# Small column tiles for the first products, and two held projections ahead of the last eight output products

## The chip, the cores and the metric

The kernel runs on one core of a Trainium2 chip. The metric is the device time of one execution in microseconds (us); of several executions the median is given. The core has a matrix engine (TensorE, PE in the profile; PEld are its weight loads), VectorE (DVE), ScalarE (ACT), GpSimd (POOL) and SyncE (SP), which here issues most transfers. Each engine works through a list of instructions of its own, in order, and waits on semaphores for the others. Products write to PSUM, which DVE and ACT read.

## The reference

The input x has 2,048 tokens of 640 values. It is layer-normalised, and the result feeds two branches, whose product is added to x:

```python
xn = _layernorm(x, axis=-1)
s = _A_ref(xn, A_wq, A_wk, A_wv, A_wo, A_beta)     # attention with a memory
g = _silu(_B_ref(xn, B_w_gate, B_w_up, B_w_down))  # gated linear unit, F = 1536
return x + s * g
```

Branch A projects xn to q, k and v (32 heads of 20), and goes through four segments of 512 tokens. In a segment each head has causal softmax attention within the segment, and reads a memory that sums phi(k) v over the earlier segments; the two are mixed by a gate for each head, and the heads are projected by wo. Branch B is (sigmoid(xn w_gate) * (xn w_up)) w_down.

## The kernel before

The work goes by the four segments. For each there are the Q, K and V projections, the scores and their exponentials, the attention products, the memory, 12 gate and 12 up products of 128 columns of F each (`do_gate`, `do_up`), and the down projection in eight items (`do_down`: a block j of 128 tokens by a half of the 640 columns; 12 products that accumulate in a tile `yp`, then a Tanh on ACT and a DVE instruction at L449 that leaves `aa`, the silu). The output projection is in eight pieces of the same kind (five products over chunks c of 128 of the attention output `oT`, in a tile `sp`); a DVE instruction multiplies it with `aa`, and another adds x.

The order of instructions is written by the program itself, on the host: slots with due times (`TIMES`), and a list of dense work (`dense`) from which `step` takes one product at a time to fill the slots. `do_down` is a generator, and each `next` issues one product. Products of 32 columns of weights (`tile_position`) are used in some slots: four of them, one for each quarter of the columns, take the place of a full product (L128 instead of L124).

Tiles in PSUM with the tag "d" (`yp`, `sp`, `po`, `gp`, `up` and others) come from one pool, `ps_d`, of four buffers that are given out in turn. So a tile can be written only when the reader of the tile four allocations before it is done.

*The start.* `keep_warm(9)` issues nine products of zeros, `warm` (named `mn` in the profile), into a tile `wps` that nobody reads. Behind them on PE are the transposes of the first 128 tokens (`first_transpose`, L650), which wait for their normalised row `xn` on DVE; DVE and ACT compute mean, variance, root and `xn` for the four blocks of 128 tokens as these land. The transposes of the second block (L257) and the V projections follow.

*The end.* The last two items of the down projection of the last segment (j = 3, both halves) are kept back in `held`; held[1] is the first half and held[0] the second. The last chunk of `oT` is put together late: `tail_T4` transposes a part of the attention output on PE (`po`, two products), copies it on ACT (L517) and adds the other part, `o6`, on DVE (L518), for two token blocks at a time. The chunk before it is complete only after a transfer (`tail_load`, L507) and a DVE addition at L481. Nine products of the first held item are issued, then `tail_T4(0, 2)`, the item's last three products, two output pieces (`tail_piece`, L525 and L527), and the addition and store of block 0 (`tail_add`, L533 and L536). Then the same with the second held item and `tail_T4(2, 4)`, and then the other six pieces. POOL adds blocks 0 and 2, DVE blocks 1 and 3; SP issues the stores of blocks 0, 1 and 3, ACT those of block 2.

Of the kernel before, what the change touches and what calls it, by code (L numbers as in the profile page):

```python
# [15 lines left out]
L = 512  # L16
# [59 lines left out]
def kernel(  # L76
# [14 lines left out]
    nc = tc.nc  # L91
# [56 lines left out]
    warm = stg.tile([P, 3 * L], BF, name="mn")  # L148
# [98 lines left out]
    def ln_tiles(n):  # L247
        mv = lnp.tile([P, 4, 2], F32, name="mv")
        rs = lnp.tile([P, 4], F32, name="rs")
        return mv, rs  # L250
# [202 lines left out]
    def finish(steps):  # L453
        for _ in steps:
            pass
# [54 lines left out]
    def tail_T4(j0, j1):  # L510
        po = ps_d.tile([P, 2, P], BF, name="po", tag="d")
        for j in range(j0, j1):
            nc.tensor.transpose(po[:, j - j0, :], seg[NSEG - 1]["odot"][:, j, C4:D], ident[:])
        t = slice(j0 * P, j1 * P)
        oT = seg[NSEG - 1]["oT"][:, DC - 1, t]
        pf = po[:].rearrange("p j t -> p (j t)")
        nc.scalar.copy(oT[HALF:P, :], pf[HALF:P, :])  # L517
        nc.vector.tensor_tensor(oT[0:HALF, :], pf[0:HALF, :], o6[:, t], op=ALU.add)  # L518

    def tail_piece(j, half):  # L520

        s, hs = seg[NSEG - 1], slice(half * HD, (half + 1) * HD)
        sp = ps_d.tile([P, HD], F32, name="sp", tag="d")
        for c in range(DC):
            nc.tensor.matmul(sp[:], lhsT=s["oT"][:, c, j * P:(j + 1) * P], rhs=Wo[:, c, hs],  # L525
                             start=(c == 0), stop=(c == DC - 1), skip_group_check=True)
        nc.vector.tensor_tensor(s["aa"][j][:, hs], s["aa"][j][:, hs], sp[:], op=ALU.mult)  # L527

    def tail_add(j, h0, h1, eng, queue=None):

        hs = slice(h0 * HD, h1 * HD)
        xr = xt_of[NSEG - 1][:, j, hs]
        eng.tensor_tensor(xr, seg[NSEG - 1]["aa"][j][:, hs], xr, op=ALU.add)  # L533
        if queue is not None:
            t0 = (4 * (NSEG - 1) + j) * P
            queue.dma_start(o2[t0:t0 + P, hs], xr)  # L536
# [86 lines left out]
    wps = ps_d.tile([P, L], F32, name="wps", tag="d")  # L623

    def keep_warm(k):
        for _ in range(k):
            nc.tensor.matmul(wps[:], lhsT=warm[:, 0:P], rhs=warm[:, 0:L], start=True, stop=True)

    keep_warm(9)
    mv, rs = ln_tiles(0)  # L630
    new_seg(0)
    xns, sts = {}, {}
# [110 lines left out]
    held = [dense.pop() for _ in range(2)]  # L743
# [13 lines left out]
    for p in range(0, OLD, 5):  # L757
        n, g = units[p][0], units[p][1][0][0]
# [130 lines left out]
    def fill(want):  # L889
        while done < want and (cur[0] is not None or dense and may(dense[0][0])):  # L890
            step()
# [26 lines left out]
        if cur[0] is not None and cur[0][0] * cur[0][1] < TIMES["rest"]:  # L918
            complete()
    fill(1e12)  # L920
    for _ in range(9):
        next(held[1][3])
    tail_T4(0, 2)
    finish(held[1][3])
    tail_piece(0, 0)
    tail_piece(0, 1)
    tail_add(0, 0, 2, nc.gpsimd, nc.sync)
    for _ in range(9):
        next(held[0][3])
    tail_T4(2, 4)  # L930
    finish(held[0][3])
    tail_piece(1, 0)
    tail_piece(1, 1)
    tail_add(1, 0, 1, nc.vector)
# [38 lines left out]
```

## Time and profile before

| | us |
|---|---|
| median of 3 executions | 317.38 |
| lowest, highest | 317.27, 318.7 |
| the profiled execution, whole | 319.06 |
| its span, first to last instruction | 317.3 |
| PE busy in the span | 307.3 |
| ACT, DVE, POOL busy | 226.8, 224.8, 133.9 |
| first product of zeros | 1.24 |
| first transposes | 5.26 |
| first output piece of the tail | 305.07 |
| last store issued | 314.71 |

The profiled execution is one of its own, 1.68 us above the median. The span lies within its time; 1.76 us are around it. Times in the views of the profile count from the first instruction. A row of the timeline has the start, the time from the first start to the last end, the engine, the line, the operation with its tiles, the number of instructions and, in brackets, how long the engine stood idle before and what ended that. Products overlap in the pipeline: a single one of 320 columns takes 0.30 us from start to end, but the next one starts well before.

### The profile page before, as it was taken

To read this page: it belongs to the slowest core of one execution; us is meant where nothing else is said; L and a number is where in the kernel's file an instruction comes from. 1 tells how busy PE (TensorE), PEld (TensorE's weight loads), DVE (VectorE), ACT (ScalarE), POOL (GpSimd) and SP (SyncE) were. 2 spreads that over 40 slices of the span, in tenths; PEclk is the share of its full clock that TensorE was granted. 3 is DMA by queue.
4 is the path that set the end of the run, shared out by engine and by line. 5 is a ranking of instruction groups with operands and counts; after the bars stand their busy time and mean duration, and the time that the engine had idled before them with its cause. 6 is when DMAs were issued, how large, how long until landed. Compare 5 with 4: busy or idle time off the path is not lost.

```text
span 317.3 us, 10105 instructions
## 1 busy us (share of the span) xinstructions
PE 307.3 (97%) x4239; PEld 165.8 (52%) x4268; DVE 224.8 (71%) x507; ACT 226.8 (71%) x228; POOL 133.9 (42%) x231
## 2 busy tenths in 40 slices
PE   7999999999999999999999999999999999999985
PEld 2544445665445445654665455544466645445663
DVE  5474445665868988888778999788777777634565
ACT  3724477778798776777997869678896766777620
POOL 2870035535263445335443354454443353535312
PEclk9999999999999999999999999999999999999999
DMA  7984885420851362405953385137523001250202
GB/s 251 365 325 148 301 216 164 117 53 2 217 154 58 100 166 106 105 23 160 253 163 97 111 144 146 44 118 214 168 83 119 19 23 44 105 127 0 88 20 83
DMA packets 55245, 41.26 MB, mean 130 GB/s; under 512 B 25952, under 2 KB 53824, under 8 KB 55200
## 3 DMA queue, kind: packets, MB, share of 16 engines
q1 hardware_dynamic: 52656, 35.87, 39.5%
q10 hardware_dynamic: 2544, 4.75, 4.0%
q8 instruction: 33, 0.54, 0.7%
q14 instruction: 12, 0.10, 0.1%
HBM read 19.98 MB, written 14.73 MB: 109 GB/s over the span
## 4 chain that ended last, share of the span: by engine, by line
PE 91%; DMA 3%; DVE 2%; issue 1%; ACT 1%; SPq 0%; ACTq 0%
PE up L124 11%; PE gp L124 10%; PE psq L124 10%; PE yp L124 8%; PE Sps L541 8%; PE gp L128 6%; PE yp L128 6%; PE up L128 6%; PE ApsT L565 5%; PE psv L124 5%; PE psq L128 4%; PE sp L124 3%; PE sp L128 3%; PE psv L128 2%; PE sp L525 1%
## 5 line engine op out<-in xcount | busy, mean ns | idle before, releaser
L549 ACT ACTIVATE pt<-Sps 128x2048 bf16<-128x2048 f32 x80 | 150.3, 1878 | 40.8 <-PE Sps L541 40.0
L551 POOL TENSOR_SCALAR_AFFINE_SELECT pt<-pt 128x512 bf16<-128x512 bf16 x128 | 82.8, 662 | 156.7 <-ACT pt L549 156.7
L432 DVE SCALAR_TENSOR_TENSOR hT<-tg,up 128x512 bf16<-128x512 bf16 x48 | 32.6, 678 | 23.9 <-PE up L124 10.0
L124 PE MATMUL up<-xnT,Wu 128*128 128x512 bf16 x146 | 40.3, 380 | 1.4 <-issue 1.1
L124 PE MATMUL gp<-xnT,Wg 128*128 128x512 bf16 x146 | 38.9, 379 | 0.6 <-issue 0.5
L124 PE MATMUL yp<-Wd,hT 128*128 128x320 bf16 x246 | 38.5, 299 | 0.4 <-issue 0.4
L421 ACT ACTIVATE tg<-gp 128x512 bf16<-128x512 f32 x48 | 28.5, 595 | 14.3 <-PE gp L124 10.0
L541 PE MATMUL Sps<-QT,KT 23*128 23x384 bf16 (+3 forms) x512 | 31.8, 301 | 0.1
L124 PEld LDWEIGHTS <-hT 128*128 128x128 bf16 x246 | 22.7, 98 | 11.9 <-issue 3.6
L573 DVE STREAM_TRANSPOSE tb<-ApsT 128x512 f32<-128x512 f32 x31 | 22.0, 711 | 4.3 <-PE ApsT L565 4.2
L128 PE MATMUL gp<-xnT,Wg 128*32 128x512 bf16 x352 | 24.4, 380 | 0.0
L449 DVE SCALAR_TENSOR_TENSOR aa<-t,yp 128x320 bf16<-128x320 bf16 x32 | 15.3, 477 | 12.4 <-ACT t L448 12.2
L565 PE MATMUL ApsT<-pt,V 128*32 128x512 bf16 (+2 forms) x496 | 23.5, 299 | 0.0
L124 PEld LDWEIGHTS <-Wu 128*128 128x128 bf16 x159 | 14.2, 98 | 17.4 <-issue 4.0
L124 PEld LDWEIGHTS <-Wg 128*128 128x128 bf16 x152 | 14.1, 98 | 15.8 <-issue 1.9
L128 PE MATMUL yp<-Wd,hT 128*32 128x320 bf16 x552 | 21.9, 300 | 0.0
L128 PE MATMUL up<-xnT,Wu 128*32 128x512 bf16 x324 | 21.7, 380 | 0.0
L541 PEld LDWEIGHTS <-KT 23*128 23x128 bf16 x512 | 9.1, 92 | 23.5 <-issue 23.2
L585 DVE STREAM_TRANSPOSE obT<-ob 128x256 f32<-128x256 f32 x31 | 13.5, 434 | 11.1 <-POOL ob L582 11.1
L582 POOL TENSOR_TENSOR ob<-tb,rb 128x320 bf16<-128x320 f32 x27 | 19.9, 737 | 2.3
L124 PE MATMUL psq<-xnT,Wq 128*128 128x512 bf16 x82 | 19.4, 379 | 0.2
L124 PE MATMUL psv<-Wv,xnT 128*128 128x320 bf16 x115 | 18.6, 299 | 0.4 <-ACT xnT L655 0.2
(122 smaller groups left out, 441.0 us busy)
## 6 DMA issues: line engine op xcount, KB each, us to landing
KT<-Kd SPq DMA_DIRECT2D x32, 80.0 KB
QT<-Qd SPq DMA_DIRECT2D x32, 80.0 KB
out_dram<-xt SPq DMA_DIRECT2D x14, 160.0 KB
Wg<-in_B_w_gate_dram ACTq DMA_DIRECT2D x1, 1920.0 KB
Wu<-in_B_w_up_dram ACTq DMA_DIRECT2D x1, 1920.0 KB
xt<-in_A_x_dram SPq DMA_DIRECT2D x3, 640.0 KB
Wd<-in_B_w_down_dram SPq DMA_DIRECT2D x1, 1920.0 KB
Xd<-xn SPq DMA_DIRECT2D x12, 160.0 KB
```

The source lines that it names most:

```text
L124: nc.tensor.matmul(out_, lhsT=lhsT, rhs=rhs, start=start, stop=stop, skip_group_check=True)
L128: nc.tensor.matmul(out_[cols], lhsT=lhsT[:, cols], rhs=rhs, start=start, stop=stop, tile_position=(0, 32 * r), skip_group_check=True)
L421: nc.scalar.activation(tg[:], gp[:], ACT.Tanh, scale=0.5)
L432: nc.vector.scalar_tensor_tensor(out=h[:], in0=seg[n]["tg"][:], scalar=1.0, in1=up[:], op0=ALU.add, op1=ALU.mult)
L449: nc.vector.scalar_tensor_tensor(out=s["aa"][j][:, hs], in0=t2[:], scalar=1.0, in1=yp[:], op0=ALU.add, op1=ALU.mult)
L541: nc.tensor.matmul(Sps[:, r, c0:c0 + ncol], lhsT=KT[32 * r:32 * r + DH + 3, g, kb * P:(kb + 1) * P], rhs=QT[32 * r:32 * r + DH + 3, g, q0: ...
L549: nc.scalar.activation(pt[:, :, 0:ntot], Sps[:, :, 0:ntot], ACT.Exp, scale=SCALE)
L551: nc.gpsimd.affine_select(out=pt[:, :, c0:c0 + P], in_=pt[:, :, c0:c0 + P], compare_op=ALU.is_ge, fill=0.0, base=0, pattern=[[0, 4], [1, P ...
L565: nc.tensor.matmul(ps[32 * r:32 * r + 32, q0:L], lhsT=Vflat[n % 2][:, off:off + 32], rhs=t[:, r, c0:c0 + ncol], start=(i == 0), stop=(i == ...
L573: nc.vector.transpose(tb[:].rearrange("p h e -> p (h e)"), ps[:].rearrange("p (a t b) -> p a b t", t=32, b=2))
L582: eng.tensor_tensor(to, of, by, op=ALU.mult)
L585: nc.vector.transpose(s["obT", g // 4][:, g % 4, :].bitcast(F32), ob[:].rearrange("p a e b -> p (a e b)").bitcast(F32))
```

## The change

At the start the nine full products are replaced by 17 rounds of four products. Each of the four has 32 columns of the zero weights, streams 256 columns and writes its own 32 rows of `wps`. The one full product later on (`keep_warm(1)`) stays.

At the end both held items are completed, each with its `tail_T4`, before the first output piece. The held item that was first stays first. The eight pieces, the additions and the stores keep their order among themselves.

```diff
-    keep_warm(9)
+    def keep_warm_columns(k, n):
+        for _ in range(k):
+            for r in range(4):
+                nc.tensor.matmul(wps[32 * r:32 * r + 32, 0:n], lhsT=warm[:, 32 * r:32 * r + 32], rhs=warm[:, 0:n],
+                                 start=True, stop=True, tile_position=(0, 32 * r), skip_group_check=True)
+
+    keep_warm_columns(17, L // 2)
...
     fill(1e12)
-    for _ in range(9):
-        next(held[1][3])
-    tail_T4(0, 2)
-    finish(held[1][3])
+    for k in (1, 0):
+        for _ in range(9):
+            next(held[k][3])
+        tail_T4(2 - 2 * k, 4 - 2 * k)
+        finish(held[k][3])
     tail_piece(0, 0)
     tail_piece(0, 1)
     tail_add(0, 0, 2, nc.gpsimd, nc.sync)
-    for _ in range(9):
-        next(held[0][3])
-    tail_T4(2, 4)
-    finish(held[0][3])
     tail_piece(1, 0)
     tail_piece(1, 1)
```

## The prediction

> **What bounds the kernel now.** I read the page first, then the chain of waits, then the timeline at both ends of the execution, because the change touches only the first five microseconds and the last thirteen. The page's busy shares and slices:
>
> ```profile
> span 317.3 us, 10105 instructions
> PE 307.3 (97%) x4239; PEld 165.8 (52%) x4268; DVE 224.8 (71%) x507; ACT 226.8 (71%) x228; POOL 133.9 (42%) x231
> PE   7999999999999999999999999999999999999985
> ```
>
> TensorE (PE) is the bound: its slices are full but for the first and the last two. Something is to be had only there, and at most what PE stands idle. At the start (timeline of the first microseconds; columns: start, duration, engine, line, operation):
>
> ```profile
> 1.24 3.69 PE L627 MATMUL wps<-mn 128*128 128x512 bf16 x9 [1.24 <-DVE mn L149]
> 3.77 0.15 PEld L627 LDWEIGHTS <-mn 128*128 128x128 bf16 x1 [0.28 <-issue]
> 4.20 0.15 PEld L627 LDWEIGHTS <-mn 128*128 128x128 bf16 x1 [0.28 <-issue]
> 5.26 0.45 PE L650 MATMUL pT<-ident,xn 128*128 128x128 bf16 x5 [0.32 <-DVE xn L243]
> 6.05 0.49 DVE L637 BATCH_NORM_STATS2 st<-xt 128x6 f32<-128x320 bf16 x1 [0.21 <-DMA xt<-in_A_x_dram]
> 6.66 0.15 DVE L659 RECIPROCAL rs<-rs 128x1 f32<-128x1 f32 x1
> 7.35 0.45 PE L257 MATMUL pT<-ident,xn 128*128 128x128 bf16 x5
> ```
>
> The weight loads of the nine products come 0.43 us apart: 512 columns at half rate. The transposes at 5.26 take (0.45 - 0.22)/4 = 0.056 us each, which is full rate, so the rate doubled between 4.2 and 5.26. Products ahead of 5.25 do nothing for the result: the first transposes wait for xn, and the chain of waits through this stretch runs over the landing of an x tile at 6.03, DVE's statistics and xn to the transposes at 7.35.
>
> The end (timeline of the last microseconds):
>
> ```profile
> 304.67 0.57 PE L124 MATMUL yp<-Wd,hT 128*128 128x320 bf16 x3
> 305.07 0.57 PE L525 MATMUL sp<-Wo,oT 128*128 128x320 bf16 x3
> 305.76 0.43 DVE L481 TENSOR_TENSOR oT<-oT,oTm 128x512 bf16<-128x512 bf16 x1 [1.43 <-DMA oT<-OTd]
> 306.11 0.48 DVE L449 SCALAR_TENSOR_TENSOR aa<-t,yp 128x320 bf16<-128x320 bf16 x1
> 306.25 0.31 PE L525 MATMUL sp<-Wo,oT 128*128 128x320 bf16 x1 [0.60 <-DVE oT L481]
> 306.50 0.28 DVE L518 TENSOR_TENSOR oT<-po,o 64x256 bf16<-64x256 bf16 x1
> 306.70 0.47 DVE L449 SCALAR_TENSOR_TENSOR aa<-t,yp 128x320 bf16<-128x320 bf16 x1
> 306.83 0.99 PE L525 MATMUL sp<-Wo,oT 128*128 128x320 bf16 x6 [0.28 <-DVE oT L518]
> 307.66 1.39 PE L124 MATMUL yp<-Wd,hT 128*128 128x320 bf16 x9
> 309.40 4.24 PE L525 MATMUL sp<-Wo,oT 128*128 128x320 bf16 x30
> 313.00 0.49 DVE L527 TENSOR_TENSOR aa<-aa,sp 128x320 bf16<-128x320 bf16 x1 [0.19 <-PE sp L525]
> 314.38 0.33 DVE L533 TENSOR_TENSOR xt<-aa,xt 128x320 bf16<-128x320 bf16 x1
> ```
>
> The first output product (sp) does three of its five chunks and then stands: chunk 3 waits for a DMA and L481, chunk 4 for L518. Behind it on PE's queue is the second held down projection (yp, the nine at 307.66), which waits for nothing there. The end is then PE to 313.0, two DVE pairs (L527, L533), the last store issued at 314.71, and 2.6 us until the span ends.
>
> **The change at the start.** Removed: nine full products. Added: 17 sets of four products, each 32 columns wide, streaming 256 columns; PE gets 118 more instructions, the other queues none. What a set costs: in the middle of the kernel the same form runs, and 68 yp products in 32-column tiles take 2.49 us, which is (2.49 - 0.30)/16 = 0.137 us per set of four, against (1.39 - 0.30)/8 = 0.136 for one full product. The four run beside each other. At half rate a set of 256 columns is therefore half of the measured 0.427 us, 0.213; 17 sets are 3.63 us and end their streaming at 1.24 + 3.63 = 4.87. Nine full ones at half rate would have been 3.84, to 5.08. With the rate rising as before, somewhere in 4.2 to 5.26, both end sooner. Either way PE waits for xn until 5.25: cost nothing, with 0.38 us of cover. A further 0.35 us of delay would still be covered for the chain: the transposes' ACT copy stands ahead of the root of the second row (ACT 6.01 to 6.31), and DVE asks for that root at 6.66. Bounds: from below nothing, since the landing at 6.03 sets the chain whatever PE does; from above, if the four of a set ran one after another at half rate, 68 x 0.213 = 14.5 us, against which the measured 0.137 per set speaks; I take nothing.
>
> What it could touch is the clock. For column tiles as such the trace has a row: from 102.7 to 106.9 us PE runs only 32-column products and 23-row scores, is busy 4.20 of 4.20 us, and the granted clock is 1.00. That is holding the rate, not raising it; no row shows column tiles raising it.
>
> **The change at the end.** PE's order was: nine yp of the first held item, two transposes (po), three yp, sp(0,0), sp(0,1), nine yp of the second, two po, three yp, six sp. Now the second item goes in front of all eight sp. Work on PE is the same; what changes is who waits. A po takes 0.056, a yp or sp 0.136 (sp: (4.24 - 0.30)/29), results stand 0.30 after the last product's start, and a waiting engine starts 0.03 to 0.05 after its releaser. The tiles rotate over four PSUM buffers, so each allocation waits for the reader of the fourth before it.
>
> - Second item's nine yp start at 305.07 instead of the first sp (their buffer was free: sp(0,0) used it without a wait): 9 x 0.136, to 306.30.
> - The second pair of po takes the buffer that sp(0,1) had. Its last reader is L449 of the last planned down item, which stands on DVE behind L481's wait for the DMA and ends at 306.59. po waits, from 306.30 to 306.64, a new wait of 0.34 us; behind it on PE are the three yp: 306.75 to 307.16.
> - ACT: L517 of the second pair from 306.95 to 307.32 and the Tanh to 307.79; DVE: L518 second pair 307.35 to 307.63 (needs ACT's copy), L449 second item 307.82 to 308.31. DVE has nothing else to do then; L527 of sp(0,0) stands behind it and starts about 308.2, where before it ran at 307.18.
> - sp(0,0) takes the first held item's buffer: L449 of that item ends at 307.17, so sp starts at 307.22 (0.06 of waiting). Chunks 3 and 4 have been ready since 306.2 and 306.8. The third sp needs L449's end 308.31 at 308.58, the fifth L527's end 308.7 at 309.94: no more waits.
> - 40 sp at 0.136 run without a gap. The seventh one, sp(3,0), ends at 307.22 + 34 x 0.136 + 0.30 = 312.14, where it ended at 309.40 + 24 x 0.136 + 0.30 = 312.96. L527 starts at 312.17 instead of 313.00.
> - Behind it the same pairs on DVE and the same stores: last store issued at 313.88 instead of 314.71. POOL's first add slides from 308.43 to about 309.3 and its store on SP to 310.7, and its last two end about 312.9 with ACT's store behind them, 0.9 us ahead of the last one on SP. DVE from 307.82 on has at most nine of 0.49 and four of 0.35, 5.8 us of the 6.1 to 313.88. Neither is the end.
>
> Sum: 313.00 - 312.17 = **0.83 us gained**, which is 1.2 us of idle PE removed (305.48 to 306.25 and 306.39 to 306.83) and 0.4 added. On the profiled execution (span 317.3, 319.06 in all) that gives 318.2; the median of the runs is 317.38, 1.68 below the profiled one, and I take the same difference off it: 317.38 - 0.83 = **316.6**. Bounds of this step: if the last oT chunk lands 1.2 us earlier in a run without a profile, PE had no wait to remove and the gain is nothing; if the new po wait goes and the old ones are as shown, it is 1.2. A loss is excluded by the unchanged work of PE. The value taken is that of the trace's own landing.
>
> **Rivals.**
>
> *The tail gains nothing* (earlier landing, or the new waits eat it): 317.4. For it: the timed runs are 1.7 us below the profiled one, and some of that may be shorter waits here. Against: the wait for the oT landing is two DMA trips in a row, 3.45 and 1.66 us.
>
> *The rate rises late.* The stretch of products at half rate is 3.63 us instead of 3.84, and in tiles. If the rate then stays at half until 8.6, PE's stream from 5.25 to there (10 transposes, one full product, 10 V products: 0.56 + 0.22 + 1.36 = 2.1 us) doubles, of which 1.2 us falls into its idle time: +0.9, 317.5. The trace shows 1.24 to at least 4.2 at half rate, so a window of over 3 us is needed, and the new stretch is only a little longer than that. The Trainium skill, TensorE: Matmul & The Clock Gate, Part 1, says the rate goes up after a busy window of about 3.4 us that runs free of the kernel's start, so a 3.63 us stretch could miss it in more executions than a 3.84 us one. By that rule the trace agrees (over 3 us at half rate here), and an estimate from its figures would be 0.21/3.4, some 6 more executions in 100, too few to move a median. The third run shown (318.7, 1.3 above the others) may be such an execution; two of three of them would put the median near 317.9.
>
> *Column tiles don't raise the rate at all*, the slower case: PE stays at half rate until it has been gapless with full products as long as it was before the rise (some 3.2 us: the nine end at 4.93, earlier than half rate to the last would have it) counted from 8.6, where its gaps end: 3.2 us at half rate does 1.6 us of work, +1.6 and the +0.9 from above: 316.6 + 2.5 = 319.1. It decides for slower by over 0.5% (318.97) when half rate lasts beyond 11.6. Against it: the 4.2 us of tiles at clock 1.00.
>
> *Faster by over 0.5%* (under 315.8) needs 0.75 us more than the sum; only a start where the old products miss the rise in most runs would give it, and two of the three runs lie within 0.11 us of the lowest.
>
> **Numbers.** Forecast 316.6 as worked out, 0.58 (its own range 316.2 to 317.0); tail gains nothing, 0.10; rate late, or median among late runs, 0.14 (317.5 to 317.9); not raised, 0.10 (319 and more); faster than 315.8, 0.08. About 0.5% is what a measurement of this kernel tells from no change, since the runs shown lie 0.45% apart: faster 0.09, same 0.79, slower 0.12. Range 315.9 to 318.0: below, the 1.2 bound and some scatter between runs; above, the late rate with no gain in the tail.
>
> **What would show it.** Right: column products ending before 5.25 and transposes at full rate from there; yp x12 and po between 305.07 and 307.2 with one wait of PE for DVE L449 near 306.3; 40 sp in one stretch; last store 0.8 us earlier. Wrong: products past 5.6, transposes 0.107 apart, a granted clock under 1 near the start, or a gap inside the 40 sp. The prediction falls if PE's wait before the second po is far over 0.34, or POOL's or ACT's stores end last.

## The result: slower by 0.4%, and not where the change is

| | median us | lowest to highest | runs |
|---|---|---|---|
| before | 318.44 | 317.27 to 320.48 | 22 |
| after | 319.76 | 318.79 to 321.54 | 22 |

The ratio is 1.0039, with a 95% interval of 1.0021 to 1.0057: slower by 1.3 us where 0.8 us of gain were forecast, and outside the range. The time of before is itself 1.1 us higher over 22 runs than over the three that were shown; counted from those three, the same ratio would give 318.6 us, still outside. The page of the profiled execution of after:

```profile
span 319.0 us, 10222 instructions
PE   7999999989999999899999999999999999999995
q8 instruction: 34, 0.56, 0.7%
```

The queue's row on the page of before:

```profile
q8 instruction: 33, 0.54, 0.7%
```

The last slice but one of PE is full now (9, where before has 8), as the new tail should make it; the last stays at 5. But two slices in the middle, at about 70 and 130 us, are 8 where before's are 9, and the span is 1.7 us longer. The queue q8 has 34 packets of 16 KB, one more than in before. They are taken to be the loads of PE's instructions: PE has 8,507 products and weight loads in before, and 33 times 256 are 8,448.

The start of after (timeline; start, duration, engine, line, operation):

```profile
1.24 3.82 PE L632 MATMUL wps<-mn 128*32 128x256 bf16 x68 [1.24 <-DVE mn L149]
5.30 0.71 PE L656 MATMUL pT<-ident,xn 128*128 128x128 bf16 x5 [0.24 <-DVE xn L243]
6.43 0.49 DVE L643 BATCH_NORM_STATS2 st<-xt 128x6 f32<-128x320 bf16 x1 [0.54 <-DMA xt<-in_A_x_dram]
```

The column products end before 5.25 us as forecast: a last one of 0.42 us taken off, 16 rounds take 3.40 us, 0.213 each. The transposes are at half rate here ((0.71 - 0.31)/4 = 0.10 us each); the record of the granted clock has its rise at 6.92 us, against 4.47 in before. It costs this execution nothing: the chain waits for the x tile, which landed 0.38 us later than in before, and DVE and POOL add 0.2. From here on, the lag is how much later an instruction of PE starts than the same one in the profile of before. From 14 us on it is 0.57 us.

The tail of after, with the last transpose of the attention output on DVE (L585) ahead of it:

```profile
302.69 0.45 DVE L585 STREAM_TRANSPOSE obT<-ob 128x256 f32<-128x256 f32 x1
307.18 0.42 DVE L481 TENSOR_TENSOR oT<-oT,oTm 128x512 bf16<-128x512 bf16 x1
307.60 1.79 PE L124 MATMUL yp<-Wd,hT 128*128 128x320 bf16 x12
309.23 0.27 PE L513 MATMUL po<-ident,odot 128*128 128x128 bf16 x2
309.75 5.60 PE L525 MATMUL sp<-Wo,oT 128*128 128x320 bf16 x40
316.10 0.32 DVE L533 TENSOR_TENSOR xt<-aa,xt 128x320 bf16<-128x320 bf16 x1
```

The same transpose in before:

```profile
299.76 0.45 DVE L585 STREAM_TRANSPOSE obT<-ob 128x256 f32<-128x256 f32 x1
```

Forty sp stand in one stretch, and the last addition starts 1.72 us later than in before, while the transpose starts 2.93 us later. So the tail gained 1.2 us in this pair of profiles, and 2.4 us were lost between 14 and 300 us, where no instruction differs. The normalised blocks xn are stored to DRAM (Xd) and read back transposed (xnT) for the next segment, and that is where the time goes. The places, in the timeline of after:

```profile
60.28 0.50 DVE L243 TENSOR_SCALAR xn<-xt,mv,rs 128x640 bf16<-128x640 bf16 x1 [2.24 <-DMA Xd<-xn]
69.61 0.82 PE L124 MATMUL psq<-xnT,Wk 128*128 128x512 bf16 x2 [0.94 <-DMA xnT<-Xd]
128.19 0.45 DVE L243 TENSOR_SCALAR xn<-xt,mv,rs 128x640 bf16<-128x640 bf16 x1 [1.82 <-DMA Xd<-xn]
128.55 0.68 DVE L432 SCALAR_TENSOR_TENSOR hT<-tg,up 128x512 bf16<-128x512 bf16 x1
129.28 0.81 PE L124 MATMUL up<-xnT,Wu 128*128 128x512 bf16 x3 [1.30 <-DVE hT L432]
```

The same instructions in before, where none of them waits:

```profile
57.39 0.41 DVE L243 TENSOR_SCALAR xn<-xt,mv,rs 128x640 bf16<-128x640 bf16 x1
67.96 1.24 PE L124 MATMUL psq<-xnT,Wk 128*128 128x512 bf16 x4
124.63 0.36 DVE L243 TENSOR_SCALAR xn<-xt,mv,rs 128x640 bf16<-128x640 bf16 x1
126.25 0.82 PE L124 MATMUL up<-xnT,Wu 128*128 128x512 bf16 x3
```

At 60.28 DVE has waited for the store of an earlier xn to land (the pool has two xn buffers). So the last blocks are stored late and xnT starts late, and at 69.61 PE waits for it; the lag goes from 0.57 to 1.67 us. At 128.19 DVE waits for a store once more, hT stands behind it on DVE, and PE behind hT for a PSUM buffer: the lag goes to about 3.0. The chain of waits shows the transfers (start, duration):

```profile
55.89 4.30 DMA Xd<-xn
61.49 1.75 DMA Xd<-xn
63.25 6.31 DMA xnT<-Xd
124.11 4.06 DMA Xd<-xn
```

The same kind of store, 160 KB, takes 1.75 us once and over 4 twice. A transfer lands in sixteen parts, and their times tell why it is late: of the sixteen parts of the store issued at 55.89, fifteen are there by 57.67 and the last at 60.19; of that at 124.11, fifteen by 125.86 and the last at 128.16; of xnT, fifteen by 67.97 and the last at 69.57. In before all sixteen parts of the corresponding stores are there within 1.8 us of the issue. And in each of the three an instruction load of PE starts in between: at 57.0, 125.2 and 67.6 us. The DMA view of after from 124 to 129 us:

```profile
GB/s 0 61 307 430 379 134 0 72 358 500 338 93 0 0 0 0 20 307 328 410 164 0 0 10 10 10 10 10 20 31 174 379 410 318 72 20 0 0 0 0
q8 instruction: 1, 0.02, 2.1%
```

The third burst of some 400 GB/s ends, and 10 GB/s go on for most of a microsecond, which fits one late part of 10 KB. In the window of the same work in before (121 to 127 us) there is no instruction packet and no such tail; its loads start at 120.6 and 131.1.

### The profile page after: what moved, and what is told of

Read it like the earlier page. It is cut to its first block, busy times and chain, and to the rows that moved or that the text cites. A ratio compares the mean times of both kernels' runs of the same rounds, so it can differ in the third digit from the quotient of the medians.

```text
span 319.0 us, 10222 instructions
## 1 busy us (share of the span) xinstructions
PE 308.1 (97%) x4297; PEld 167.8 (53%) x4327; DVE 226.1 (71%) x507; ACT 226.7 (71%) x228; POOL 134.7 (42%) x231
## 4 chain that ended last, share of the span: by engine, by line
PE 86%; DMA 7%; DVE 3%; issue 1%; ACT 1%; POOL 1%; SPq 0%; DVEq 0%; ACTq 0%
PE up L124 10%; PE psq L124 10%; PE gp L124 9%; PE yp L124 9%; PE Sps L541 8%; PE gp L128 6%; PE up L128 5%; PE ApsT L565 5%; PE psv L124 5%; PE yp L128 4%; PE psq L128 4%; DMA Xd<-xn 4%; PE sp L124 3%; PE psv L128 2%; DMA xnT<-Xd 2%; PE sp L128 2%
## 5 line engine op out<-in xcount | busy, mean ns | idle before, releaser
L585 DVE STREAM_TRANSPOSE obT<-ob 128x256 f32<-128x256 f32 x31 | 13.4, 433 | 11.0 <-POOL ob L582 10.9
```

Source lines behind the costliest of these rows:

```text
L585: nc.vector.transpose(s["obT", g // 4][:, g % 4, :].bitcast(F32), ob[:].rearrange("p a e b -> p (a e b)").bitcast(F32))
```

## The experiments

Three explanations were put to the test. Theory F: 118 additional instructions on PE (59 products and their weight loads) move all its instruction loads, one for 256 instructions, and some now fall on transfers that others wait for. Theory C: the column products raise the clock late. Theory T: the new order of the tail costs. All ratios are against before, run beside them.

### One part alone

e1_head_only is before with the column products (the first part of the change's diff); e2_tail_only is before with the new tail (its second part).

> Only the column products at the start; the tail stands as before. Theory F (the 118 additional PE instructions move PE's instruction loads, of 16 KB for 256 instructions each, and these fall on transfers that PE waits for): slower by some 2 us, ratio near 1.006. Theory C (column products raise the clock a window later): slower by 0.5 to 2 us, 1.002 to 1.006. Theory T (the new order of the tail is what costs): no change, 1.000.

> Only the new order of the tail; nine full products at the start as before. Theories F and C: faster by 0.8 to 1.2 us, ratio 0.996 to 0.9975, as the tail of the changed kernel's profile gains 1.2 us on that of before. Theory T: slower by 1 us or more, 1.003 and up.

Measured: e1 319.47 us, ratio 1.0044 (1.0022 to 1.0067); e2 317.54 us, ratio 0.9975 (0.9958 to 0.9993). The loss is all in the start, and theory T falls. In e2 the clock rises at 7.06 us, behind nine full products and later than in after, and at 14 us ACT's copies of V are 0.1 us ahead of before's: a rise at 7 us costs nothing there.

### The instructions without the products

`keep_warm_columns` is defined as in the change, here and below.

```diff
     keep_warm(1)
+    keep_warm_columns(14, 8)
+    for r in range(3):
+        nc.tensor.matmul(wps[32 * r:32 * r + 32, 0:8], lhsT=warm[:, 32 * r:32 * r + 32], rhs=warm[:, 0:8],
+                         start=True, stop=True, tile_position=(0, 32 * r), skip_group_check=True)
```

> Start and tail as before, nine full products, and 59 products of 8 columns in 32-column tiles behind the full product that follows the first transposes, where PE is idle: 118 instructions more, as in the change, without its products at the start. Theory F: as slow as the column products alone, near 1.006. Theory C and theory T: no change, 0.999 to 1.001.

Measured: 319.34 us, ratio 1.0034 (1.0017 to 1.0051), less than the 1.006 that theory F expected, but as slow as e1 within the intervals, with before's nine full products and a rise at 5.35 us. Theory C falls as the cause. Its chain of waits:

```profile
55.06 3.83 DMA Xd<-xn
61.89 6.19 DMA xnT<-Xd
122.62 3.33 DMA Xd<-xn
```

The same three transfers are late as in after, with instruction loads at 56.4, 66.1 and 123.5 us. The two jumps of the lag are 0.43 us near 68 and 1.05 near 128; e1 has 1.02 and 1.05 there.

### The products with whole loads more

Column products of the same total length, but 256 or 374 instructions more instead of 118; 256 is one load, 374 is one load and 118.

```diff
-    keep_warm(9)
+    keep_warm_columns(34, L // 4)
+    nc.tensor.matmul(wps[0:32, 0:8], lhsT=warm[:, 0:32], rhs=warm[:, 0:8], start=True, stop=True,
+                     tile_position=(0, 0), skip_group_check=True)
```

> Column products as in the change and of the same length in all (34 rounds of four of 128 columns, 17 x 256 = 34 x 128, and one narrow product), so that PE has 256 instructions more than before and its loads of 256 instructions fall on the same instructions as before; the tail as before. Theory F: no change, 0.999 to 1.001. Theory C: as slow as the column products of the change, 1.002 to 1.006. Theory T: no change.

e6 has `keep_warm_columns(49, 88)` in that place:

> Old tail; column products as 49 rounds of four of 88 columns, as long in all as those of the change: 374 PE instructions more than before, which is 118 and one whole load of 256. Theory F: as slow as with 118 more, ratio 1.003 to 1.006. A theory in which 118 happens to be a bad number for another reason than its rest by 256: near 1.000.

Measured: e4 318.15 us, ratio 1.0002 (0.9979 to 1.0025); e6 319.82 us, ratio 1.0065 (1.0041 to 1.0089). What counts is what is left of the number after whole loads of 256, not the number. In e4 the loads are back at 53.8, 60.8, 70.2, 120.4 and 131.0 us, where before has them at 54.1, 60.9, 70.5, 120.6 and 131.1, and the lag is -0.2 us through both places. In e6 they are at 57.4, 67.1 and 124.9, and its chain of waits has the late transfers again:

```profile
55.68 4.25 DMA Xd<-xn
63.03 6.28 DMA xnT<-Xd
123.85 3.24 DMA Xd<-xn
```

The Trainium skill (Runtime: NRT & Kernel Launch, Instruction fetch mechanics) says that an engine's instructions are loaded in 16 KiB blocks of 256, and that crossing a boundary is mostly hidden. The blocks agree (33 and 34 packets of 16 KB, and a period of 256 in these ratios). Hidden from PE they are in the next experiment, too; but not from a store that they meet, which lands 2.3 to 2.5 us late in after.

### Taking away the wait

The changed kernel with its 118 instructions, but the third and fourth xn of a segment go to a tile that is free then, so DVE needn't wait for the first two stores.

```diff
+    spare = {}
+
     def ln_norm(n, j, mv, rs):
-        xn = lnp.tile([P, D], BF, name="xn", bufs=2)
+        if n and j >= 2:
+            if j == 2:
+                spare["mn"] = stg.tile([P, 3 * L], BF, name="mn")
+            xn = spare["mn"][:, (j - 2) * D:(j - 1) * D]
+        else:
+            xn = lnp.tile([P, D], BF, name="xn", bufs=2)[:]
...
```

> The changed kernel with its 118 instructions more, in which the third and fourth normalised block of a segment (xn) go to a tile that is free at the time, so that DVE no longer waits for the stores of the first two. Theory F with the chain store of xn, DVE's wait, PE: the stalls of PE at 69.6 and 129.3 us in the changed kernel's profile (1.10 and 1.46 us) go, ratio 0.996 to 0.999. A rival in which the loads hold PE itself up: no change, 1.003 to 1.006.

Measured: 317.35 us, ratio 0.9999 (0.9979 to 1.0018). Against the changed kernel's 1.0039 that is 0.4% back, a little short of what was expected. The timeline at the second place:

```profile
123.20 1.25 PE L124 MATMUL up<-xnT,Wu 128*128 128x512 bf16 x4
124.01 0.41 DVE L250 TENSOR_SCALAR mn<-xt,mv,rs 128x640 bf16<-128x640 bf16 x1
124.49 0.37 DVE L250 TENSOR_SCALAR mn<-xt,mv,rs 128x640 bf16<-128x640 bf16 x1
126.12 0.82 PE L124 MATMUL up<-xnT,Wu 128*128 128x512 bf16 x3
```

A load starts at 123.5 us here as well, and the store that it meets has fifteen parts there by 124.07 and the last at 125.70; at 56.2 us it is the same (56.97 and 58.42). But no row has a wait: the blocks are written at once, the up products start without a gap, and the lag is -0.13 us from 12 to 167 us. So the loads reach PE through DVE's wait for the xn buffers and the late xnT behind it, and not by holding PE up.

### Both parts, with the loads back in place

e5 is the changed kernel with e4's start.

> Both parts of the change, with the column products as 34 rounds of four of 128 columns and one narrow product: 256 PE instructions more than before instead of 118. Theory F (what costs is where PE's loads of 256 instructions fall): the loss of the start is gone and the tail's gain is left, ratio 0.996 to 0.9985, faster than before and by some 2 us than the changed kernel. Rival theory N (what costs is the number of instructions, or the products in column tiles together with the new tail): as slow as the changed kernel or slower, 1.003 to 1.006.

Measured: 317.88 us, ratio 1.0007 (0.9988 to 1.0025): the loss of the changed kernel is mostly gone, but the tail's gain is not reached, and the ratio lies above what theory F expected. Its profile shows one price of the 256 that was not thought of (timeline):

```profile
8.67 0.57 PE L124 MATMUL psv<-Wv,xnT 128*128 128x320 bf16 x3 [1.17 <-DMA Wv<-in_A_wv_dram]
```

An additional load now starts at 6.6 us, among the weights (fifteen parts of a transfer of Wv are there by 7.32 us, the last at 8.63), and PE waits 1.17 us for Wv; the lag from there is 0.57 us. e6 has the same wait, 0.92 us, behind a load at 5.4; e4, with a load at 6.5, has none.

### The new xn tile with and without the new tail

e9 is e2 with e7's xn; e10 is before with e7's xn.

> Nine full products as before, the new tail, and the third and fourth xn in a tile that is free: no instruction more on PE, and neither the stores of xn nor the last transfer of oT can stall PE when a load of PE's instructions falls on them. Theory F: the best of all, ratio 0.996 to 0.998. Rival (the parts' gains don't add, since the loads seldom fall there with the old number of instructions): as the new tail alone or less, 0.998 to 1.000.

> The kernel before with only the third and fourth xn in the free tile. Theory F: with the old number of instructions no load falls on the stores of xn in the profiles, so there is next to nothing to gain, ratio 0.998 to 1.000. Rival (the wait for the xn buffers costs PE by itself, whatever the loads do): 0.996 or less.

Measured: e9 317.46 us, ratio 1.0001 (0.9980 to 1.0022); e10 317.55 us, 0.9997 (0.9983 to 1.0012). By itself the free tile gains nothing that can be told, so what e7 took back is what the loads cost. e9 misses what theory F expected. The tail explains it. From the start of DVE's last transpose ahead of the tail to the end of the last addition, the five profiles with the new tail have 13.73 or 13.74 us. Of the seven with the old one, five have 13.71 or 13.72, e8 has 14.25 and before 14.94. In those five the oT transfer is there when DVE comes to L481, 4.49 us behind the transpose; then the old order doesn't wait either. Row by row, in e1 (old tail):

```profile
305.95 0.42 DVE L481 TENSOR_TENSOR oT<-oT,oTm 128x512 bf16<-128x512 bf16 x1
306.78 1.52 PE L525 MATMUL sp<-Wo,oT 128*128 128x320 bf16 x10
309.88 4.24 PE L525 MATMUL sp<-Wo,oT 128*128 128x320 bf16 x30
```

In before and e8 L481 waits for the transfer, and in both an instruction load starts within it, at 301.8 and 303.7 us: in before all parts but one of the store of `obT` that the transfer waits for are there by 301.92, and that one at 304.01. In the other ten the loads start between 297.0 and 300.4, about when that store is issued or earlier, or at 307.7 and later. The stall that the forecast was going to remove was such a meeting itself.

### The price of the clock

```diff
-    keep_warm(9)
+    keep_warm_columns(34, 8)
+    nc.tensor.matmul(wps[0:32, 0:8], lhsT=warm[:, 0:32], rhs=warm[:, 0:8], start=True, stop=True,
+                     tile_position=(0, 0), skip_group_check=True)
```

> Old tail; at the start 137 products of only 8 columns in 32-column tiles, so that PE has 256 instructions more but is busy for only a microsecond or two before the first transposes: the price of a clock that rises late. Theory C with the prices of the prediction: +0.9 to +2.5 us, ratio 1.003 to 1.008. Rival: what PE does ahead of 11 us waits for transfers and DVE anyway, 0.999 to 1.002.

Measured: 320.48 us, ratio 1.0083 (1.0056 to 1.0110), just above what theory C expected. The clock's record has the rise at 12.13 us, and the lag at 14 us is 2.68. The timeline:

```profile
1.24 1.26 PE L632 MATMUL wps<-mn 128*32 128x8 bf16 x136 [1.24 <-DVE mn L149]
5.34 0.71 PE L658 MATMUL pT<-ident,xn 128*128 128x128 bf16 x5 [2.83 <-DVE xn L243]
7.66 0.49 DVE L645 BATCH_NORM_STATS2 st<-xt 128x6 f32<-128x320 bf16 x1 [1.73 <-DMA xt<-in_A_x_dram]
8.40 0.71 PE L124 MATMUL psv<-Wv,xnT 128*128 128x320 bf16 x2 [1.00 <-DVE xnT L661]
8.95 0.72 PE L257 MATMUL pT<-ident,xn 128*128 128x128 bf16 x5
```

PE is busy for 1.26 us and idle for 2.83, and the transposes at 8.95 are still at half rate. But they are 1.60 us behind before's for another reason: DVE at 7.66 waits for an x tile, of which fourteen parts are there by 5.56 us and the last at 7.63, against 6.03 in before, and one of the loads starts at 5.3. So 1.6 of the 2.7 us are a late tile; the other 1.1 came up behind it, while PE ran at half rate until 12.13. Whether the timed executions had the late tile is not on record, and no run shows the price of the clock alone.

## Why the prediction was wrong

**The step that failed** is the sentence on the start, "PE gets 118 more instructions, the other queues none", with its cost of nothing. It counted what the instructions do on PE and not that they are loaded: 118 instructions move every later load of 256 by that much. The three that met the xn stores and xnT in after came some 3 to 6 us earlier (60.9 to 57.0, 70.5 to 67.6, 131.1 to 125.2). e1, e3 and e6 (118 by the rest) lie at 1.0034 to 1.0065, e4 (256) at 1.0002, and e7 takes the loss back by taking the wait away. That the late part of a store lies on the same DMA engine as the load is inferred from the one part in sixteen; no record here names the engine.

**The products themselves** were costed right: 0.213 us a round, an end before 5.25, no cost by their form. The rise was late in after, 6.92 us, but with full products it stands at 4.47, 5.35, 7.06, 5.08 and 3.98, and with tiles of full length at 6.92, 6.43, 5.89, 3.96, 3.78 and 6.27. Either form raises the clock, and neither in a fixed place. The rival that it would not be raised at all is out. Its price, +2.5 us, is not confirmed by the 2.7 of e8, since 1.6 of those are a late x tile: that the two are close is luck. No profile has a rise near 8.6, so the +0.9 for that stays open. The transposes at half rate, one of the prediction's signs of being wrong, did show in after, at no cost.

**The tail** went as described but for the wait before the second po, which did not come, since the transfer landed early. The mis-sized term is the gain: 0.83 us were read from one profile in which a load had met the transfer; 1.2 were measured in that pair of profiles, and nothing where the transfer is on time (13.73 against 13.71 us). The prediction took the 0.83 off the median, though its profile was 1.68 us above the median, and the stall makes up 1.2 us of its tail against the five old tails without it. By the times the new order gains 0.25% in e2 against before, and nothing that can be told in three other pairs (1.0039 and 1.0044, 1.0007 and 1.0002, 1.0001 and 0.9997). The prediction's own lower bound, and its rival "the tail gains nothing" with a chance of 0.10, had the condition right: a transfer that lands earlier.

**Same, faster or slower:** the move of 0.39% lies within the 0.5% band that had 0.79, but on the other side, and no rival had the mechanism. The range was made from the two ends of the kernel alone.

No version beat both kernels clearly; e2 has the one interval below 1, and e9, with the same tail and more, does not confirm it. Open is how the loads' times scatter between executions (the last one at 301.8 us in before and 300.0 in e4, on the same instructions), and why the median of before itself was 318.4, 318.2, 317.5 and 317.7 in the four comparisons (the second ran on another chip than the last two).

## What to carry to other kernels

In these runs an instruction added to PE's queue moved all of its instruction loads behind it: before a change of some dozens of instructions is costed at nothing, look at when the loads come, one for 256, and which transfers stand there that somebody waits for. An unexplained loss in a part that did not change is tested by adding idle instructions up to a whole load, though the additional load can meet something itself, as in e5; and a buffer more where an engine waits for a store to land takes the dependence away. A stall of one profile is worth what it costs in most executions, so look at a second one before a reordering is built on it.

## What the hardware did that had not been expected

- Where a load of 16 KB, 1 to 2 us long, started within a 160 KB store, one sixteenth of the store landed 2.3 to 2.5 us late (57.67 to 60.19, 125.86 to 128.16 in after; 1.4 to 1.7 us in e7), with the other parts on time; q8 has 0.7% of the DMA time.
- The clock's rise stood anywhere from 3.8 to 7.1 us after the first instruction with products from 1.24 to about 5 us, and at 12.1 with 1.3 us of them. Up to 7.1 it cost nothing that the V projections' copies show; at 12.1 the lag was 2.7 us, 1.6 of it a late x tile.
